# Retention and a token-mixing MLP on one core: a table-driven order, its engines, banks and load forms written anew

## The chip, the cores and the metric

The kernel runs on one core of a Trainium2 chip. The metric is the device time of the kernel in microseconds. Before the change the median of three runs is 100.91 us (100.23, 100.91 and 100.99).

## What is computed

Four batches of 768 tokens, eight heads of 64 channels. The first half is retention, a decayed recurrent attention; the second a mixing MLP whose token-mixing weights come from the tokens themselves:

```python
state = gamma * state + k[t] (outer) v[t]          # per head, gamma_h = 1 - 2**(-5-h)
y[t]  = (1/8) * q[t] @ state                       # retention
x     = y, heads side by side                      # (batch, 768, 512)
wq, wk = x @ w_q, x @ w_k                          # 64 wide
mixed = (wq @ wk.T / 8) @ x                        # per batch, no softmax
out   = relu(mixed) @ w_out
```

## The kernel before

The work is cut into 12 *pairs*: a pair is two chunks of 128 tokens of one batch, three pairs make a batch. Within a pair retention is computed by chunks: products of q and k under a causal mask (the decay is put into v and into the output as row factors), plus q times the state that the earlier chunks left. The mixing is reassociated: z = wk^T x is summed over the three pairs of a batch, then mixed = wq z, so a batch's mixing waits for its three pairs.

All five engines are scheduled by hand. One table, ORDER, is a list of tokens that a loop at the kernel's end turns into instructions, so the order of tokens is the order of each engine's own queue. A token `name.pair.part:E@banks=slot` names the step, the engine E (A = ACT, V = DVE, P = POOL; steps without it run on PE) and the PSUM banks. A semaphore wait is made where a step reads what another engine or a DMA writes, or overwrites what is still read; each engine works through its queue strictly in order. The steps of a pair:

- Lk, Lq, Lv (L172 to L193): load k, q, v (512 KB each, fp32) into one of 27 staging slots; all but half of the first v are issued by SP. LW and LO load the MLP's weights; S stores.
- ck, cq, cv (L351, L408, L375): cast k and q to bf16, and multiply v by its decay factor into bf16 (cv, on POOL).
- trk, trq, xt (L448, L505, L710): PE transposes into PSUM, as eight 128x128 ones into one bank or, with two banks named, sixteen 64-row ones. ek, eq, exT copy the result to SBUF.
- sc, eat (L533, L568): PE scores of one half of the heads, then DVE multiplies by the mask.
- st, es (L585, L601): PE adds k^T v of a chunk to the state in bank 7; es copies the state to SBUF. A chunk's st must wait until es has read the state before it.
- in, ia, ex (L623, L661, L694): PE adds q times state and scores times v; DVE scales by the decay into x.
- wqk, ew, zm, ez, mx (L744 to L798): the two small projections (matmuls at L748 and L759), their copy, z, its copy, and the mixing.
- r, pj, eo (L814, L823, L835): relu of one chunk, projection by w_out (four matmuls at L826), copy into a staging slot.
- fill (L345) puts matmuls on zeros into PE's queue where it would stand idle.

KINDS gives each pair's layout of k and v. "R": two neighbouring tokens lie side by side in a partition (512-byte rows); the cast then sorts chunks into partition halves, so ck takes two 64-partition instructions for each chunk, and cv too. "2" keeps the two tokens side by side: ck and cv are one 128-partition instruction for each part, but sc, in and ia need twice the PE instructions, on quarters of the array (L544, L641, L652). "M": k as in R, v loaded as 256-byte rows, four DMAs for each pair (L185), so that cv is one 128-partition instruction for each chunk. Before, pairs 1, 2 and 6 are "2" and pairs 9, 10 and 11 "M".

BUFS gives the number of buffers of each tile. A step that takes a new tile waits until all readers of the one it replaces are done. relu had four tiles of one chunk each.

Of the kernel before, what the change touches and what calls it, by code (L numbers as in the profile page):

```python
# [22 lines left out]
Lq.10=5 cv.3.1:P cq.5.0:P ia.0.1@56 fill.1@1 trk.2@1 fill.1@3 in.0.1@56 Lk.10=12 cq.2.1:A cq.2.0:A
sc.1.0@23 ek.2:V cv.4.0:P sc.1.1@01 trq.2@4 eq.2:A es.0.1:A ia.0.0@56 eat.1.0:V ex.0:V eat.1.1:V
cv.4.1:P fill.4@2 sc.2.1@34 cq.3.0:A cv.5.0:P sc.2.0@56 fill.2@2 st.1.0 es.1.0:A ck.3.0:A ck.3.1:A
Lv.10=6 Lq.11=8 ia.1.1@01 in.1.1@01 st.1.1 eat.2.1:V ck.6.0:P ia.1.0@01 in.1.0@01 trq.3@4 eat.2.0:V
xt.0@5 cv.5.1:P ex.1:V cq.7.1:P cq.7.0:P cv.6.1:P es.1.1:V exT.0:V eq.3:V trk.3@6 fill.2@2 in.2.0@01
cv.6.0:P Lv.11=9 st.2.0 ck.4.1:A ek.3:A xt.1@5 es.2.0:A exT.1:V ck.4.0:A ia.2.1@01 ia.2.0@01
in.2.1@01 ck.7.1:P ex.2:V st.3.0 fill.1@2 sc.3.0@56 trk.4@34a cq.4.1:A cv.7.1:P cv.7.0:P W:A trq.4@0
xt.2@1 ek.4:V sc.3.1@23 ck.8.1:P cq.8.0:P eat.3.0:V eq.4:V wqk.1@4 ew.1:V cq.5.1:A exT.2:A es.3.0:A  # L30
wqk.0@5 ck.8.0:P sc.4.0@01 trq.5@6 wqk.2@4 ck.5.1:A ew.0:A eat.4.0:V ew.2:V zm.0.0@5 sc.4.1@01
st.3.1 eat.3.1:V ck.5.0:A WO.0:A es.3.1:A trk.5@4 cq.9.1:P cv.8.0:P in.3.1@23 zm.0.1@5 ia.3.1@23
ia.3.0@23 eat.4.1:V ez.0:V cv.9.0:P cv.8.1:P st.4.0 ex.3:V ek.5:A es.4.0:A in.4.0@01 mx.0@45
in.4.1@01 ia.4.1@01 ia.4.0@01 eq.5:V WO.1:A st.4.1 xt.3@23a r.0.1:A pj.0.1@6 ex.4:V r.0.0:A es.4.1:A
ck.6.1:A eo.0.1:A=11 xt.4@01a cv.9.1:P mx.1@45 exT.3:V r.1.0:A cq.6.0:A sc.5.0@23 pj.0.0@6 st.5.0
exT.4:V r.1.1:V eat.5.0:V trk.6@4 ek.6:V sc.5.1@01 cq.6.1:A eo.0.0:A=11 trq.6@56a wqk.4@2 es.5.0:A
ia.5.0@34 eq.6:A in.5.0@34 in.5.1@34 eat.5.1:V trq.7@56a mx.2@01 ew.4:V eq.7:V r.2.1:A r.2.0:A
ck.7.0:A ia.5.1@34 wqk.3@2 ex.5:V pj.1.0@5 sc.6.1@01 st.6.0 eo.1.0:A=14 sc.6.0@34 xt.5@6 trk.7@5
ek.7:A eat.6.1:V pj.1.1@0 exT.5:V wqk.5@6 es.6.0:V st.6.1 eo.1.1:A=14 ew.5:A es.6.1:A ew.3:A
# [6 lines left out]
cv.11.0:P cq.10.1:A xt.6@12a in.8.1@34 in.8.0@34 mx.5@56 eq.9:A cv.11.1:P ia.8.0@34 ia.8.1@34
wqk.7@0 exT.6:V r.5.0:A r.5.1:A sc.9.0@12 sc.9.1@56 cq.10.0:A ex.8:V eat.9.0:V st.9.0 trq.10@3
ew.7:A pj.5.0@0 trk.10@12a wqk.6@4 eat.9.1:V ia.9.0@56 ia.9.1@56 ck.11.1:A es.9.0:A S.3 ek.10:V
eo.5.0:A=18 eq.10:A in.9.1@56 xt.8@01a sc.10.1@23 st.9.1 exT.8:A ew.6:V pj.4.1@4 trk.11@0 es.9.1:A
ex.9:V wqk.8@1 eat.10.1:V trq.11@23a ek.11:A sc.10.0@56 st.10.0 ew.8:A zm.2.0@0 es.10.0:A  # L50
eo.4.1:A=16 eq.11:V eat.10.0:V zm.2.1@0 ez.2:A st.10.1 xt.9@12a sc.11.1@34 pj.5.1@0 eat.11.1:V
exT.9:A es.10.1:A ia.10.0@56 mx.6@12 sc.11.0@34 eat.11.0:V in.10.1@56 in.10.0@56 eo.5.1:A=18 st.11.0
r.6.0:A ia.10.1@56 pj.6.0@0 r.6.1:A ex.10:V es.11.0:A ia.11.1@34 ia.11.0@34 eo.6.0:A=17 in.11.0@34
in.11.1@34 mx.8@12 xt.10@56a r.8.0:A exT.10:A S.4 r.8.1:V wqk.9@0 pj.8.1@1 mx.7@56 S.2 ex.11:V
ew.9:A eo.8.1:V=19 xt.11@23a exT.11:A pj.8.0@0 wqk.10@1 eo.8.0:A=19 ew.10:A wqk.11@2 ew.11:V r.7.1:V
S.1 pj.6.1@0 zm.3.0@1 eo.6.1:A=17 zm.3.1@1 ez.3:V r.7.0:V pj.7.1@2 mx.9@01 mx.11@34 mx.10@56
eo.7.1:A=21 r.9.1:V pj.7.0@2 r.9.0:A pj.9.1@0 r.10.0:A pj.9.0@1 S.8 S.5 eo.7.0:A=21 r.11.1:A
pj.11.1@2 S.6 eo.9.0:V=22 r.11.0:A r.10.1:A pj.10.1@6 S.7 S.9.0 pj.11.0@1 eo.10.1:V=20 eo.9.1:A=22
eo.11.1:A=23 pj.10.0@0 eo.10.0:A=20 eo.11.0:V=23 S.9.1 S.11.1 S.10.1 S.11.0 S.10.0
""".split()  # L60

KINDS = "R22RRR2RRMMM"
FIRST = ('v', 0, 0)
SLOTS = 27
U = 8
PAD = 224
SPLIT = ()
# [9 lines left out]
def kernel(  # L77
# [270 lines left out]

    def ck(e, b, p, c):  # L351
        st = pairs[p]
        if KINDS[p] in "2H":
            if "ks" not in st:
                st["ks"] = new("ks", [128, HP, 2, 2, D])
            copy(
                e,
                st["ks"][:, :, :, c],
                st["k_st"].rearrange("p (hp x j d) -> p hp x j d", hp=HP, x=2, j=2)[:, :, c],
            )  # L360
            return
        if "ks" not in st:
            st["ks"] = new("ks", [128, 2, HP, 2, D])
        if KINDS[p] == "N":
            copy(
                e,
                st["ks"][:, c].rearrange("p hp x d -> p (hp x d)"),
                st["k_st"][:, 512 * c : 512 * c + 512],
            )
            return  # L370
        src = st["k_st"].rearrange("p (h j d) -> p h j d", j=2, d=D)
        for j in range(2):
            copy(e, st["ks"][rows(j), c].rearrange("p hp x d -> p (hp x) d"), src[rows(c), :, j])
# [31 lines left out]
                op=ALU.mult,  # L405
            )

    def cq(e, b, p, x):  # L408
        st = pairs[p]
        if U == 8:  # L410
            if "qs" not in st:
                st["qs"] = new("qs", [128, U, 2, D])
            copy(e, st["qs"][:, :, x], st["q_st"].rearrange("p (x u d) -> p x u d", x=2, u=U)[:, x])
# [90 lines left out]

    def trq(e, b, p):  # L505
        st = pairs[p]
        qs = st["qs"]
        ident = ident_q if U == 8 else identity
        srcs = [(None, u) for u in range(U)] if U == 8 else [(hp, u) for hp in range(HP) for u in range(U)]
# [12 lines left out]
    def eq(e, b, p):  # L522
        st = pairs[p]
        st["qT"] = new("qT", [128, 2, HP, C])
        b = st["qtr"]
        if len(b) == 1:
            copy(e, st["qT"].rearrange("p c hp t -> p (c hp t)"), bank16(b[0]))
        else:
            copy(e, st["qT"].rearrange("p c hp t -> p c (hp t)"), two16(b))
# [281 lines left out]
                )  # L811
        st["mx_ps"] = ps

    def r(e, b, p, c):  # L814
        st = pairs[p]
        st["relu", c] = new("relu", [128, 2, 2, C])
        src = st["mx_ps"][:, :, :, c * C : c * C + C]
        if e == "A":
            nc.scalar.activation(out=st["relu", c], in_=src, func=ACT.Relu)  # L819
        else:  # L820
            nc.vector.tensor_relu(out=st["relu", c], in_=src)  # L821

    def pj(e, b, p, c):  # L823
        st = pairs[p]
        for a in range(NDM):
            nc.tensor.matmul(  # L826
                out=bank32(b[0]),
                lhsT=st["relu", c][:, a // 2, a % 2, :],
                rhs=wout_sb[:, a, :],
                start=(a == 0),  # L830
                stop=(a == NDM - 1),
# [69 lines left out]
```

## Time and profile before

| | us |
|---|---|
| median of three runs | 100.91 |
| the profiled execution, its own time | 100.14 |
| its span in the profile | 98.4 |
| PE busy | 88.6 |
| DVE busy | 74.4 |
| ACT busy | 70.3 |
| POOL busy | 51.8 |

The profiled execution is 1.7 us longer than its span: that lies around the span and no engine's work is in it. Busy times of PE are those of pipelined matmuls, whose ends overlap the next one's start; what a step costs PE is better read from the chain of waits, where each piece begins where the one before ends. The granted clock is 0.996 over the span. In the profile, a row names line, engine, operation, output and inputs; "[0.89 <-DMA stage<-in_v_dram]" says that the engine stood idle for 0.89 us before the row and that a load of v ended the wait. SPq rows are DMA issues and last as long as SP is held by them.

### The profile page before, as it was taken

Reading aid. Unit: us, or ns where it says so; the run is one execution under the profiler, and the core shown is the slowest. Engines: PE = TensorE matmul, PEld = TensorE weight load, DVE = VectorE, ACT = ScalarE, POOL = GpSimd, SP = SyncE. Lnnn points to the kernel's source line nnn. Section 1 sums busy time; section 2 is a strip of 40 time slices with the busy share of each in tenths; the row PEclk is TensorE's granted clock in tenths of the full one; section 3 lists DMA queues with packets and bytes.
Section 4 is the critical chain, followed back from the end, with each engine's and each line's share of the span. In section 5 each row is a group of like instructions: output and inputs, shape, how many; then the busy total and the mean of one; then the engine's idle time right before and its main releaser. Section 6 shows DMA issues by size and latency. Waiting matters only on the chain.

```text
span 98.4 us, 3827 instructions
## 1 busy us (share of the span) xinstructions
PE 88.6 (90%) x1626; PEld 59.9 (61%) x1642; DVE 74.4 (76%) x127; ACT 70.3 (71%) x124; POOL 51.8 (53%) x68
## 2 busy tenths in 40 slices
PE   5994899999869999999999988999999989999940
PEld 1333477487757776586887554786787766744410
DVE  6697689999792999998769897888958964460440
ACT  4237573689799979967589967899579776339620
POOL 6082319176385989989977999497990000000000
PEclk9999999999999999999999999999999999999998
DMA  1999999999998999999899799799905910690893
GB/s 26 282 385 368 367 363 361 343 327 282 293 330 256 303 317 348 354 336 293 255 337 309 177 323 323 159 244 273 361 21 205 402 46 0 245 391 14 323 397 132
DMA packets 37953, 26.73 MB, mean 272 GB/s; under 512 B 8240, under 2 KB 31792, under 8 KB 37936
## 3 DMA queue, kind: packets, MB, share of 16 engines
q1 hardware_dynamic: 37408, 26.22, 84.5%
q10 hardware_dynamic: 528, 0.26, 0.9%
q8 instruction: 13, 0.21, 0.8%
q14 instruction: 4, 0.03, 0.1%
HBM read 20.19 MB, written 6.29 MB: 269 GB/s over the span
## 4 chain that ended last, share of the span: by engine, by line
PE 55%; SPq 20%; ACT 7%; DMA 6%; DVE 4%; issue 2%; POOL 1%; DVEq 0%; POOLq 0%
PE banks L826 19%; SPq L193 11%; DMA stage<-in_q_dram 6%; SPq L172 6%; PE banks L748 5%; PE banks L759 5%; PE banks L558 3%; PE banks L685 3%; SPq L200 3%; ACT relu L819 3%; PE banks L592 2%; PE banks L515 2%; PE banks L804 2%; DVE relu L821 2%; PE banks L631 2%
## 5 line engine op out<-in xcount | busy, mean ns | idle before, releaser
L401 POOL TENSOR_TENSOR vs<-stage,fv 64x512 bf16<-64x512 f32 x22 | 23.6, 1075 | 6.4 <-DMA stage<-in_v_dram 5.2
L576 DVE TENSOR_TENSOR at<-banks,maskR 128x1024 bf16<-128x1024 f32 x18 | 21.7, 1219 | 3.8 <-PE banks L558 3.8
L826 PE MATMUL banks<-wout_sb,relu 128*128 128x512 bf16 x84 | 22.9, 381 | 0.9 <-DVE relu L821 0.2
L147 ACT CAST ks<-stage 64x512 bf16<-64x512 f32 (+1 forms) x25 | 15.4, 618 | 4.7 <-DMA stage<-in_k_dram 4.3
L147 ACT COPY stage<-banks 128x512 f32<-128x512 f32 x19 | 11.0, 587 | 5.8 <-PE banks L826 5.7
L706 DVE TENSOR_TENSOR x<-banks,fy 128x1024 bf16<-128x1024 f32 x12 | 14.6, 1219 | 0.6 <-PE banks L685 0.3
L826 PEld LDWEIGHTS <-relu 128*128 128x128 bf16 x96 | 8.3, 99 | 9.3 <-issue 0.8
L148 POOL CAST ks<-stage 64x512 bf16<-64x512 f32 (+1 forms) x15 | 9.1, 609 | 6.4 <-DMA stage<-in_k_dram 5.8
L347 PE MATMUL banks<-warm 128*128 128x512 bf16 x34 | 10.9, 451 | 1.6 <-DVE warm L226 1.2
L819 ACT ACTIVATE relu<-banks 128x512 bf16<-128x512 f32 x18 | 10.0, 601 | 3.0 <-PE banks L804 1.5
L147 ACT CAST qs<-stage 128x512 bf16<-128x512 f32 x14 | 8.4, 618 | 1.5 <-DMA stage<-in_q_dram 1.3
L382 POOL TENSOR_TENSOR vs<-stage,fv 128x512 bf16<-128x512 f32 x6 | 6.2, 1047 | 5.4 <-DMA stage<-in_v_dram 5.4
L576 DVE TENSOR_TENSOR at<-banks,mask 128x1024 bf16<-128x1024 f32 x6 | 7.1, 1219 | 1.0 <-ACT ks L147 0.8
L147 ACT COPY kT<-banks 128x1024 bf16<-128x1024 bf16 x6 | 6.1, 1011 | 2.4 <-PE banks L473 1.7
L759 PE MATMUL banks<-wqk_w,xT 128*128 128x64 bf16 x96 | 7.5, 243 | 0.1
L558 PE MATMUL banks<-qT,kT 64*128 64x128 bf16 x144 | 6.8, 218 | 0.9 <-ACT kT L147 0.5
L347 PEld LDWEIGHTS <-warm 128*128 128x128 bf16 x38 | 3.8, 110 | 6.0 <-issue 3.0
L147 ACT CAST s<-banks 128x256 bf16<-128x256 f32 x16 | 6.0, 375 | 1.9 <-PE banks L592 1.9
L748 PE MATMUL banks<-xT,wqk_w 128*128 128x256 bf16 x48 | 7.3, 275 | 0.0
L148 DVE COPY qT<-banks 128x1024 bf16<-128x1024 bf16 x8 | 5.5, 686 | 2.0 <-PE banks L515 1.0
L148 POOL CAST qs<-stage 128x512 bf16<-128x512 f32 x9 | 5.4, 611 | 2.8 <-DMA stage<-in_q_dram 2.5
L592 PE MATMUL banks<-vs,ks 128*64 128x64 bf16 (+1 forms) x200 | 6.9, 198 | 0.0
(81 smaller groups left out, 153.4 us busy)
## 6 DMA issues: line engine op xcount, KB each, us to landing
stage<-in_k_dram SPq DMA_DIRECT2D x12, 512.0 KB, 7.4
stage<-in_q_dram SPq DMA_DIRECT2D x12, 512.0 KB, 6.6
out_dram<-stage SPq DMA_DIRECT2D x9, 512.0 KB, 4.0
stage<-in_v_dram SPq DMA_DIRECT2D x8, 512.0 KB, 7.8
stage<-in_v_dram SPq DMA_DIRECT2D x12, 128.0 KB, 5.2
out_dram<-stage SPq DMA_DIRECT2D x6, 256.0 KB, 2.2
stage<-in_moe_w_out_dram SPq DMA_DIRECT2D x4, 256.0 KB, 4.8
stage<-in_v_dram ACTq DMA_DIRECT2D x1, 256.0 KB, 4.3
```

The costliest lines, as they stand in the source:

```text
L147: return nc.scalar.copy(out=out, in_=in_)
L148: return ENGINES[e].tensor_copy(out=out, in_=in_)
L193: eng.dma_start(out=to[g, hs], in_=fr[g, hs])
L347: nc.tensor.matmul(out=bank32(b), lhsT=warm[:, 0:128], rhs=warm, start=True, stop=True)
L401: eng.tensor_tensor(out=st["vs"][rows(j), c].rearrange("p hp x d -> p (hp x) d"), in0=src[rows(c), :, j], in1=fv[rows(c), cp, :, j].to_bro ...
L558: nc.tensor.matmul(out=at[:, x, hi, c], lhsT=kT[rows(x), hp, c], rhs=qT[rows(x), c, hp], start=(hi == 0 and c == 0), stop=(hi == 1 and c = ...
L576: ENGINES[e].tensor_tensor(out=st["at", half].rearrange("p x hi j t -> p x (hi j t)").rearrange("p x (n f) -> p x n f", n=n), in0=st["at_p ...
L706: ENGINES[e].tensor_tensor(out=dst, in0=src, in1=f.to_broadcast([128, 2, H, D]), op=ALU.mult)
L748: nc.tensor.matmul(out=ps[:, 128:384], lhsT=wqk_sb[:, a, 0 : 2 * DH], rhs=st["xT"][:, a].rearrange("p c t -> p (c t)"), start=(a == 0), st ...
L759: nc.tensor.matmul(out=wk[:, c], lhsT=st["xT"][:, a, c, :], rhs=wqk_sb[:, a, 2 * DH :], start=False, stop=(a == NDM - 1), skip_group_check ...
L819: nc.scalar.activation(out=st["relu", c], in_=src, func=ACT.Relu)
L826: nc.tensor.matmul(out=bank32(b[0]), lhsT=st["relu", c][:, a // 2, a % 2, :], rhs=wout_sb[:, a, :], start=(a == 0), stop=(a == NDM - 1),)
```

## The change

Four things change.

1. ORDER is another table: the order of steps on all engines, the engine of many steps, the PSUM banks, the order of loads, the slots, and the number and places of the fillers (43 for 38).
2. KINDS: pair 1 alone is "2"; pair 2 is "R"; pairs 6 and 7 are "M" like 9, 10 and 11. Pairs 0, 3, 4, 5 and 8 stay "R".
3. ck, cq and r may take both parts in one instruction. It is used for ck of pair 1 and cq of pairs 2, 7 and 9 on POOL, cq of pairs 1, 4, 5 and 6 on ACT, and r of pairs 1, 3, 4, 7 and 8 on ACT.
4. relu becomes one tile for a whole pair, and there are two of them.

A switch QF (transposing q in fp32) is added and left empty.

```diff
-fill.15@6 cv.0.0:V Lk.0=1 ck.0.1:V Lq.0=2 ck.0.0:A Lq.1=3 Lk.1=4 Lk.2=5 Lq.2=6 Lv.1=7 fill.3@0
...
+fill.15@6 Lk.0=1 cv.0.0:V ck.0.0:P Lq.0=2 cq.0.0:V cv.0.1:P Lk.1=3 ck.0.1:A Lq.1=4 Lq.2=5 Lk.2=6
+Lv.1=7 Lq.3=8 fill.7@0 trk.0@0 ek.0:V Lv.2=9 ck.1:P cq.0.1:A Lk.3=10 st.0.0 trq.0@1 eq.0:V fill.3@2
...
-KINDS = "R22RRR2RRMMM"
+KINDS = "R2RRRRMMRMMM"
...
-    ks=6, vs=6, qs=4, kT=3, qT=3, at0=2, at1=2, s=4, x=6, xT=3, m=7, z=2, relu=4,
+    ks=6, vs=6, qs=4, kT=3, qT=3, at0=2, at1=2, s=4, x=6, xT=3, m=7, z=2, relu=2,
...
-    def ck(e, b, p, c):
+    def ck(e, b, p, c=None):
...
+            if c is None:
+                copy(
+                    e,
+                    st["ks"].rearrange("p hp j x d -> p hp x j d"),
+                    st["k_st"].rearrange("p (hp x j d) -> p hp x j d", hp=HP, x=2, j=2),
+                )
+                return
...
-    def cq(e, b, p, x):
+    def cq(e, b, p, x=None):
...
+            if x is None:
+                copy(
+                    e,
+                    st["qs"].rearrange("p u x d -> p x u d"),
+                    st["q_st"].rearrange("p (x u d) -> p x u d", x=2, u=U),
+                )
+                return
...
-    def r(e, b, p, c):
-        st = pairs[p]
-        st["relu", c] = new("relu", [128, 2, 2, C])
-        src = st["mx_ps"][:, :, :, c * C : c * C + C]
+    def r(e, b, p, c=None):
+        st = pairs[p]
+        if "relu" not in st:
+            st["relu"] = new("relu", [128, 2, 2, 2 * C])
+        ts = slice(0, 2 * C) if c is None else slice(c * C, c * C + C)
+        dst, src = st["relu"][:, :, :, ts], st["mx_ps"][:, :, :, ts]
...
-                lhsT=st["relu", c][:, a // 2, a % 2, :],
+                lhsT=st["relu"][:, a // 2, a % 2, c * C : c * C + C],
```

Three places of the new order follow, as the built programs have it. The first is DVE at its first real work, after the constants. (vs, ks and qs are the bf16 tiles of v, k and q, kT and qT the transposed ones, at the masked scores, x the retention's output.) Before:

```order
L401 TENSOR_TENSOR vs_206<-stage_110,fv_158 64x512 x2
L148 CAST ks_210<-stage_110 64x512 x2
L148 CAST qs_236<-stage_110 128x8x64
L148 COPY qT_271<-banks_109 128x1024
L148 COPY kT_273<-banks_109 128x1024
L576 TENSOR_TENSOR at1_356<-banks_109,maskR_183 128x1024
```

And now:

```order
L414 TENSOR_TENSOR vs_207<-stage_110,fv_158 64x512 x2
L148 CAST qs_214<-stage_110 128x8x64
L148 COPY kT_241<-banks_109 128x1024
L148 COPY qT_264<-banks_109 128x1024
L610 TENSOR_TENSOR at0_310<-banks_109,maskR_183 128x1024
L610 TENSOR_TENSOR at1_316<-banks_109,maskR_183 128x1024
```

The cast of pair 0's k has left DVE (POOL has it now, ahead of its first product), and kT goes before qT.

The second is SP's queue of loads, from v of pair 1, the eighth tensor, on. Before:

```order
L193 DMA stage<-in_v_dram 128x8x128
L172 DMA stage<-in_q_dram 128x2x512
L193 DMA stage<-in_k_dram 128x8x128
L193 DMA stage<-in_v_dram 128x8x128
L193 DMA stage<-in_k_dram 128x8x128
L193 DMA stage<-in_v_dram 128x8x128
L200 DMA stage<-in_moe_w_q_dram 128x4x64
L200 DMA stage<-in_moe_w_k_dram 128x4x64
L172 DMA stage<-in_q_dram 128x2x512 x2
```

And now:

```order
L193 DMA stage<-in_v_dram 128x8x128
L172 DMA stage<-in_q_dram 128x2x512
L193 DMA stage<-in_v_dram 128x8x128
L193 DMA stage<-in_k_dram 128x8x128 x2
L193 DMA stage<-in_v_dram 128x8x128
L172 DMA stage<-in_q_dram 128x2x512
L200 DMA stage<-in_moe_w_q_dram 128x4x64
L200 DMA stage<-in_moe_w_k_dram 128x4x64
L193 DMA stage<-in_v_dram 128x8x128
```

v of pair 2 goes ahead of k of pair 3, and q of pair 4 ahead of the weights. Ahead of this piece, k of pair 2 went from sixth to seventh. Further on, v of pairs 6 and 7 are four DMAs each (64x8x64), the second of them the 27th tensor.

The third is ACT around the relu of pair 2. Before, with relu tiles of one chunk:

```order
L147 COPY qT_1188<-banks_109 128x1024
L819 ACTIVATE relu_1232<-banks_109 128x512
L819 ACTIVATE relu_1234<-banks_109 128x512
L147 CAST ks_755<-stage_110 64x512 x2
L147 COPY stage_110<-banks_109 128x512
```

And now, where the first of DVE's and ACT's halves takes the tile:

```order
L147 COPY stage_110<-banks_109 128x512
L855 ACTIVATE relu_1065<-banks_109 128x4x128
L147 CAST s_1069<-banks_109 128x256
L147 CAST ks_1071<-stage_110 64x512 x2
L147 CAST qs_1076<-stage_110 128x2x8x64
```

Behind pair 2's relu there now stand the copy of pair 5's state and the casts of k and q of pair 6.

More of the change, by code (lines that the diff above doesn't have):

```diff
@@ L23 @@
[L23 to L39, printed above, removed]
@@ L46 @@
[L46 to L51, printed above, removed]
@@ new lines @@
+eo.1.1:A=3 ez.1:A st.6.0 Lv.8=7 eq.8:V eat.7.1:V ek.8:V es.6.0:A mx.3@45 sc.7.0@01 in.6.1@23
+eat.7.0:V Lq.11=8 r.3:A Lk.11=10 st.6.1 ia.6.0@23 ia.6.1@23 ck.9.0:A cv.8.0:P cv.8.1:P pj.3.0@4
+sc.8.1@01 mx.5@56 eo.3.0:A=9 es.6.1:V ex.6:V Lv.9=11 st.7.0 eat.8.1:V r.5.0:V trk.9@4 es.7.0:A
+ek.9:A ck.11.0:P pj.3.1@2 xt.6@3 exT.6:V r.5.1:A ia.7.1@01 cv.9.1:P ia.7.0@01 eo.3.1:A=9 mx.4@45
+in.7.0@01 Lk.10=13 r.4:A in.7.1@01 trq.9@23a st.7.1 Lq.10=14 wqk.6@6 ex.7:V eq.9:V es.7.1:A
+cq.11.0:A cv.9.0:P ck.10.1:P ew.6:A pj.5.0@4 sc.8.0@01 xt.7@56a Lv.10=12 eo.5.0:A=16 exT.7:A
@@ L306 @@
         )
+    if QF:
+        ident_f = const_pool.tile([128, 128], FP32, name="ident_f")
+        nc.vector.tensor_copy(out=ident_f, in_=ident_q)
     def mask(name, toks):
@@ L506, in trq @@
         st = pairs[p]
+        if p in QF:
+            src = st["q_st"].rearrange("p (x u d) -> p u x d", x=2, u=U)
+            st["qtr"] = ps = two32(b).rearrange("p i (v n) -> p i v n", n=C)
+            for u in range(U):
+                nc.tensor.transpose(ps[:, u // 4, u % 4], src[:, u], ident_f)
+            return
         qs = st["qs"]
```

69 lines of the change are left out of this document (48 added, 21 removed).

## Prediction

> **What bounds the kernel now.** I read the page first: engines, slices, queues.
>
> ```profile
> span 98.4 us, 3827 instructions
> ...
> PE   5994899999869999999999988999999989999940
> ...
> DMA  1999999999998999999899799799905910690893
> ...
> q8 instruction: 13, 0.21, 0.8%
> ```
>
> PE is nearly full from the third slice on, and DMA is full for two thirds of the span. Thirteen instruction reads took 0.8% of 16 engines' span, 0.008 x 16 x 98.4 / 13 = 0.97 us each on one DMA engine, which a load split over all engines waits for. The chain of waits shows where one limit gives way to the other.
>
> ```profile
> 20.97 6.24 DMA stage<-in_q_dram
> ...
> 27.32 0.62 POOL qs L148
> ...
> 27.99 0.62 PE banks L515 x8
> ...
> 29.39 0.54 PE banks L748 x4
> ...
> 33.34 0.56 DVE m L148
> 33.90 1.14 DVE at L576
> ...
> 92.71 1.90 PE banks L826 x8
> 94.64 0.58 ACT stage L147
> ```
>
> Until 27.2 us the chain is loads: q of pair 4 lands, POOL casts it, PE transposes it (L515), and only behind that, at 29.39, starts the first L748 matmul (the hypernetwork weights, token wqk.1). From there to 94.61 the chain is nearly all PE. So I ask three things: when does wqk.1 start, how much PE work stands behind it, and what makes PE wait there.
>
> **PE work behind wqk.1.** The same view gives what each step costs PE when it is not waiting.
>
> ```profile
> 38.11 0.34 PE banks L721 x16
> ...
> 46.83 0.35 PE banks L544 x16
> ...
> 51.18 0.22 PE banks L558 x8
> ...
> 51.86 0.12 PE banks L641 x4
> 51.98 0.24 PE banks L652 x8
> ...
> 63.24 0.23 PE banks L631 x16
> ...
> 69.38 0.23 PE banks L721 x16
> ...
> 71.05 0.45 PE banks L473 x8
> ```
>
> Behind wqk.1 the tables hold the same 24 pj, 12 mx, 12 wqk and 8 zm. Pair 6 loses the two-token form: two halves of sc fall from 0.35 to 0.22 (L544 to L558), -0.26; a row of in from 0.12 + 0.24 to half of 0.23, -0.24. (Pair 2 loses it too, ahead of wqk.1, where PE runs fillers: nothing.) Four xt go from sixteen half-height transposes (0.23 and 0.34, mean 0.28) to eight full ones (0.45, as in L473): +0.68. One trq moves behind wqk.1, half-height, taken like the other 16-transpose rows at 0.23. Sum -0.26 - 0.24 + 0.68 + 0.23 = +0.4 us.
>
> **When wqk.1 starts.** These timeline rows of DVE, ACT and POOL give durations and landings (a wait on a DMA ends when it has landed).
>
> ```profile
> 5.04 2.14 DVE L401 TENSOR_TENSOR vs<-stage,fv 64x512 bf16<-64x512 f32 x2 [0.89 <-DMA stage<-in_v_dram]
> 7.19 1.61 DVE L148 CAST ks<-stage 64x512 bf16<-64x512 f32 x2
> ...
> 12.05 1.23 DVE L576 TENSOR_TENSOR at<-banks,maskR 128x1024 bf16<-128x1024 f32 x1 [0.50 <-PE banks L558]
> ...
> 16.14 1.22 DVE L576 TENSOR_TENSOR at<-banks,mask 128x1024 bf16<-128x1024 f32 x1
> 17.29 1.23 DVE L706 TENSOR_TENSOR x<-banks,fy 128x1024 bf16<-128x1024 f32 x1
> ...
> 25.93 1.23 DVE L706 TENSOR_TENSOR x<-banks,fy 128x1024 bf16<-128x1024 f32 x1 [0.24 <-PE banks L652]
> ```
>
> ```profile
> 6.54 1.25 ACT L147 CAST ks<-stage 64x512 bf16<-64x512 f32 x2 [3.42 <-DMA stage<-in_k_dram]
> ```
>
> ```profile
> 5.24 2.85 POOL L401 TENSOR_TENSOR vs<-stage,fv 64x512 bf16<-64x512 f32 x2 [2.98 <-DMA stage<-in_v_dram]
> ...
> 14.99 2.05 POOL L382 TENSOR_TENSOR vs<-stage,fv 128x512 bf16<-128x512 f32 x2 [2.21 <-DMA stage<-in_v_dram]
> ...
> 20.34 2.05 POOL L382 TENSOR_TENSOR vs<-stage,fv 128x512 bf16<-128x512 f32 x2 [2.74 <-DMA stage<-in_v_dram]
> 23.21 2.16 POOL L401 TENSOR_TENSOR vs<-stage,fv 64x512 bf16<-64x512 f32 x2 [0.82 <-DMA stage<-in_v_dram]
> ```
>
> ```profile
> L147 ACT CAST ks<-stage 64x512 bf16<-64x512 f32 x22 | 13.6, 616 | 3.7 <-DMA stage<-in_k_dram 3.4
> ...
> L147 ACT COPY kT<-banks 128x1024 bf16<-128x1024 bf16 x6 | 6.1, 1011 | 2.4 <-PE banks L473 1.7 <-PE banks L457 0.5 <-DVE at L576 0.2
> ...
> L148 DVE COPY qT<-banks 128x1024 bf16<-128x1024 bf16 x8 | 5.5, 686 | 2.0 <-PE banks L515 1.0 <-PE banks L519 1.0
> ```
>
> Loads land in queue order: k of pair 0, the second tensor, at 6.5, the eighth at 14.9, the eleventh at 20.3, the thirteenth at 23.1. Eighth less second is 8.4 / 6 = 1.4 us a tensor. From eighth to eleventh 5.4 us stand for three, 1.2 more than 4.2: one instruction read (0.97) fits. PE has 3080 rows for 3286, so twelve reads for thirteen, at most 0.97 us; I count none of it, since by PE's place in its queue the first two reads still fall among tensors ten to fourteen.
>
> Now I add rows along the new order. k of pair 0 is cast by POOL and ACT from 6.54 (1.25 each) instead of ACT and DVE, whose own 2.14 and 1.61 went first: its transposes end at 8.6, DVE's two copies (0.69 each) at 10.0, the first eat starts at 10.5 (12.05 now), and x of pair 0 at 13.4 (17.29). Then the lead is spent: k of pair 2 is seventh, 13.4, its casts end at 14.7, and PE has trk.2 and trq.2 ahead of sc.1.0, so the first eat of pair 1 starts near 16.0 (16.14). k of pair 3 has become eleventh, 20.3; ACT casts it and half of pair 4's in 3 x 1.25 to 24.05, es.1.1 stands behind, in.2.0 waits for that, and x of pair 2 starts at 25.9 (25.93). So up to here nothing is won, though early steps move by over 1.5 us. The gain comes after it: trq.4 now stands behind wqk.1, so PE doesn't wait for q of pair 4. x of pair 2 ends at 27.1, xt.2 at 27.65, one filler follows; ACT has copied xT of pair 1 by 25.2 and, after q of pair 4 (a 1024-wide cast taken at the 1.01 of a 1024-wide copy), cast the weights by 27.05. wqk.1 starts at 27.85: -1.5 us. Bounds: 0, if anything on ACT slips to where q's landing was; -2.4, if the third read falls later and k of pair 3 lands 0.97 earlier.
>
> POOL's cast of k of pair 1 in one 1024-wide piece, and q of pair 2, have no row on POOL; between 1.01 (ACT's 1024-wide copy) and twice 0.62 (the 64x512 row), taken at 1.15; either end leaves k of pair 2, landing at 13.4, as what PE waits for.
>
> Where DVE's first k cast met POOL's product, its two halves took 1.61 us (ACT's two 1.25), and POOL's two products 2.85 against 2.16 later. In the Trainium skill, "SBUF — State Buffer", section "Who interferes with whom", a DVE cast in a two-port mode and a GpSimd instruction exclude each other: the later one is blocked for the whole instruction. The trace agrees in kind. By that rule the new DVE cast of q of pair 0, at 7.8, waits for POOL's next product, 1.0 us, and the first eat of pair 1 starts at 16.4 in place of 16.0; the sum below would be -0.5 if that were carried on, and stays at -0.9 by the rows, as the wait for k of pair 3 at 20.3 comes after it.
>
> **What makes PE wait behind wqk.1.** Before, PE stands 1.7 us at 33.34 for DVE's m and at. In the new order these are done when in.3.1 and zm.0.0 come (31.6): -1.7. Smaller new waits in the same stretch, added up along the rows (mx for ez, pj for WO.0, st.5.0 for v): +0.85. The new one that I find is the relu tile: two whole tiles for two pairs, so that pair 2's r waits until both projections of pair 0 are done. ACT is in order: r.2.0 waits for pj.0.0 (near 40.0), behind it stand es.5.0, k and q of pair 6 (0.4 + 1.25 + 1.0), to 43.1, and trq.6 on PE, free at 42.1, waits for that q: +1.05. Merged casts and relus save ACT some 0.1 us each; they are inside these times. Together +0.2. Later waits I leave as they are: at the tail the last relus wait on projections just ended, about 0.1 each.
>
> **256-byte rows.** POOL saves two of four products on pair 7; the loads pay.
>
> ```profile
> 48.06 6.27 SPq L185 DMA_DIRECT2D stage<-in_v_dram  x4
> ```
>
> ```profile
> 12.00:16.00 4.00, 3.84 (x80) 2.87 (x80) 3.64 (x4) 2.77 (x4) 1.63 (x3) 1.00 1.08 372
> 54.00:57.00 3.00, 3.00 (x65) 1.85 (x65) 2.71 (x4) 2.87 (x6) 2.87 (x5) 1.00 0.80 182
> ```
>
> ```profile
> 52.16 1.26 POOL L148 CAST ks<-stage 64x512 bf16<-64x512 f32 x2 [0.96 <-DMA stage<-in_k_dram]
> ```
>
> 0.524 MB at 372 GB/s is 1.4 us, at the 182 of such a stretch 2.9: +1.5 at most, 0 at least; I take 1.3. The 27th tensor, which landed at 52.2, is now v of pair 7, behind a second such load: 54.8. Its product ends near 55.9, and st.7.0 needs it at 56.7. Hidden, by 0.8 us.
>
> **Sum.** -1.5 + 0.4 + 0.2 = -0.9 us on the profiled execution of 100.14 (span 98.4): 99.2. That run lies 0.77 below the median of three, 100.91; the same step from the median gives 100.0. I take the middle, 99.6.
>
> **Rivals.** (1) *The lead isn't there.* wqk.1 starts near 29.4, since DVE and ACT, not loads, pace the front: x of pair 2 comes out no earlier in my own sum. Then 99.6 + 1.5 = 101.1. Against it: what PE waits for at 27.99 is a load's cast. (2) *Slower: SP is held by the 256-byte rows.* Four issues kept SP 6.27 us, and what is queued behind them started late. If a load costs 6.0 instead of 2.7, v of pair 7 lands 6.6 later, the slack takes 0.8, and PE stands 5.8 at st.7.0: 105.4. It makes the kernel slower by over 1% (above 101.9) from 3.1 us of delay on. Against: SP may only have waited for room. (3) *Slower: the relu tile.* Two tiles also hold r.9 behind both projections of pair 6 and r.11 behind those of pair 10, at the end, where nothing covers PE. If each costs one projection (four L826 matmuls; the eight from 92.71 took 1.90, so 0.95), +1.9 and another 0.5 at r.2: 102.0. Against: in the order other pairs' projections stand between.
>
> **Chances.** Forecast 0.55 (own range 98.2 to 100.6), of which 0.13 falls within 1%; rival 1 0.16, within 1%, of which 0.02 slower; rival 2 0.10, rival 3 0.19, slower. A measurement can tell about 1% from no change. Faster by over 1%: 0.55 - 0.13 = 0.42; within: 0.13 + 0.14 = 0.27; slower: 0.02 + 0.10 + 0.19 = 0.31. The range leaves out rival 2's far end and the forecast's early tail: 98.2 to 102.6.
>
> **What would show it.** Right: the first L748-kind matmul near 27.9, not 29.4; x of pair 2 still near 26; ACT idle before relu of pair 2, released by PE, near 40; PE idle before the transposes of pair 6. Wrong: PE waiting on POOL's v of pair 7 or 8 (rival 2), or on ACT or DVE relu in the last 6 us (rival 3). My sums along the rows take about 0.1 us for a hand-over between engines; were it 0.2 throughout the front, the lead would go.

## The result, and the profile after

The changed kernel takes 103.75 us (median of four runs, 102.56 to 104.01) where the kernel before, beside it, takes 100.89 (100.23 to 100.99): a ratio of 1.035, interval 1.029 to 1.041. The forecast was 99.6, its range ended at 102.6, and the sign was the other one. Ratios here leave disturbed runs out, so that one of them need not be the quotient of two medians. The profiled execution took 103.8 us, its span is 102.0, and its mean granted clock 0.983 where it was 0.996.

The slices of the page, 2.55 us each, show where to look.

```profile
span 102.0 us, 3618 instructions
...
PE   5997699799999999918999999999999999999650
...
PEclk9999999999999999995899999999999999999999
DMA  1999999999999979997999995996910693267764
...
q8 instruction: 12, 0.20, 0.8%
```

PE has one hole, the 18th slice (43.4 to 45.9 us), and in the two slices behind it the granted clock is down. Windows of PE, PEld, DVE, ACT and POOL, with the clock, the DMA share and GB/s at the end of a row, put numbers to it.

```profile
42.00:44.00 2.00, 1.43 (x31) 0.97 (x32) 1.54 (x3) 0.96 (x3) 1.22 (x3) 1.00 1.06 381
44.00:46.00 2.00, 0.24 (x8) 0.12 (x7) 1.23 (x1) 1.96 (x3) 0.70 (x1) 0.94 1.09 293
46.00:48.00 2.00, 1.63 (x19) 0.93 (x21) 0.69 (x1) 1.95 (x4) 1.10 (x3) 0.50 0.80 171
48.00:50.00 2.00, 2.00 (x30) 1.39 (x30) 0.00 (x0) 1.50 (x4) 1.94 (x3) 0.70 0.81 235
50.00:52.00 2.00, 2.00 (x58) 1.68 (x51) 1.79 (x4) 1.96 (x4) 1.17 (x3) 1.00 1.11 250
```

PE is busy 0.24 us of two, then for four microseconds nearly full but at a mean clock of 0.50 and 0.70: 19 and 30 matmuls in the time in which it then does 58 (different ones, but the same L782 matmuls that take 0.60 a group elsewhere take 1.00 here). The 0.70 is a mean of two values; cut at other places, the windows show one step down and one up:

```profile
45.00:45.75 0.75, 0.00 (x0) 0.00 (x0) 0.50 (x1) 0.73 (x2) 0.46 (x1) 1.00 1.10 268
45.90:49.00 3.10, 2.63 (x22) 1.49 (x24) 0.69 (x1) 3.03 (x6) 2.14 (x4) 0.50 0.71 163
49.25:50.00 0.75, 0.75 (x25) 0.65 (x25) 0.00 (x0) 0.28 (x2) 0.75 (x1) 1.00 1.15 337
```

The timeline of PE says whom it waited for.

```profile
43.95 0.29 PE L665 MATMUL banks<-s,qT 64*128 64x64 bf16 x8 [0.52 <-ACT s L147]
46.15 0.61 PE L545 MATMUL banks<-ident_q,qs 64*128 64x64 bf16 x16 [1.91 <-ACT qs L147]
...
47.52 1.06 PE L862 MATMUL banks<-wout_sb,relu 128*128 128x512 bf16 x2 [0.22 <-issue]
48.38 1.00 PE L782 MATMUL banks<-xT,wqk_w 128*128 128x256 bf16 x4
```

The transposes of q of pair 6 (trq.6, L545) wait 1.91 us for ACT's cast. ACT's timeline shows what came before that cast, and DVE's what ACT had waited for.

```profile
39.38 0.59 ACT L147 COPY stage<-banks 128x512 f32<-128x512 f32 x1 [0.71 <-POOL vs L414]
43.04 0.60 ACT L855 ACTIVATE relu<-banks 128x512 bf16<-128x512 f32 x1 [3.07 <-DVE relu L857]
43.53 0.37 ACT L147 CAST s<-banks 128x256 bf16<-128x256 f32 x1
43.78 1.25 ACT L147 CAST ks<-stage 64x512 bf16<-64x512 f32 x2
45.05 1.04 ACT L147 CAST qs<-stage 128x1024 bf16<-128x1024 f32 x1
```

```profile
39.99 2.36 DVE L610 TENSOR_TENSOR at<-banks,maskR 128x1024 bf16<-128x1024 f32 x2
42.26 0.68 DVE L857 TENSOR_SCALAR relu<-banks 128x512 bf16<-128x512 f32 x1
```

ACT stands 3.07 us before its half of pair 2's relu, r.2.0, and it is not released by PE near 40, as the prediction had it, but by DVE's half, r.2.1. That half stands in DVE's queue behind two masks of pair 5 (2.36 us) and comes at 42.26. Behind r.2.0 on ACT are the state and the casts of k and q of pair 6 (0.37, 1.25, 1.04), exactly the queue that the prediction named.

At the end of the kernel a second new wait shows, in ACT's timeline first and then in PE's.

```profile
95.16 0.60 ACT L855 ACTIVATE relu<-banks 128x512 bf16<-128x512 f32 x1 [1.20 <-PE banks L862]
```

```profile
92.32 3.40 PE L862 MATMUL banks<-wout_sb,relu 128*128 128x512 bf16 x15 [0.23 <-DVE relu L857]
96.54 1.90 PE L862 MATMUL banks<-wout_sb,relu 128*128 128x512 bf16 x8 [0.83 <-ACT stage L147]
```

r.11.1 waits 1.20 us for the projections of pair 10, and PE then stands 0.83 us before the last eight matmuls. The front, last, came out much as it was walked. These are DVE's rows and the first projection of pair 1 on PE (wqk.1).

```profile
8.01 1.13 DVE L148 CAST qs<-stage 128x512 bf16<-128x512 f32 x1 [1.77 <-DMA stage<-in_q_dram]
...
14.10 1.23 DVE L740 TENSOR_TENSOR x<-banks,fy 128x1024 bf16<-128x1024 f32 x1
...
16.44 2.36 DVE L610 TENSOR_TENSOR at<-banks,mask 128x1024 bf16<-128x1024 f32 x2 [0.53 <-PE banks L578]
...
26.51 1.22 DVE L740 TENSOR_TENSOR x<-banks,fy 128x1024 bf16<-128x1024 f32 x1
```

```profile
28.52 0.60 PE L782 MATMUL banks<-xT,wqk_w 128*128 128x256 bf16 x4
```

k of pair 3, for which ACT waits, landed at 20.1:

```profile
20.07 3.78 ACT L147 CAST ks<-stage 64x512 bf16<-64x512 f32 x6 [1.64 <-DMA stage<-in_k_dram]
```

The same view of the kernel before has wqk.1 and the last projections here:

```profile
29.32 0.61 PE L748 MATMUL banks<-xT,wqk_w 128*128 128x256 bf16 x4
...
88.08 6.52 PE L826 MATMUL banks<-wout_sb,relu 128*128 128x512 bf16 x27
```

(The chain of waits gave 29.39 for the same start, because there a piece begins where the one before ends.) So wqk.1 starts 0.8 us earlier than before, and the loss lies wholly behind it: from there to the end of the last projection it is 98.44 - 28.52 = 69.9 us, before 94.60 - 29.32 = 65.3.

### The profile page after: what moved, and what is told of

The parts are those of the page before. It is cut to its first block, busy times and chain, and to the rows that moved or that the text cites. A ratio compares the mean times of both kernels' runs of the same rounds, so it can differ in the third digit from the quotient of the medians.

```text
span 102.0 us, 3618 instructions
## 1 busy us (share of the span) xinstructions
PE 89.7 (88%) x1524; PEld 61.1 (60%) x1539; DVE 74.4 (73%) x128; ACT 68.3 (67%) x112; POOL 54.8 (54%) x70
## 4 chain that ended last, share of the span: by engine, by line
PE 49%; SPq 34%; DMA 6%; ACT 4%; issue 3%; DVE 1%; ACTq 0%
SPq L193 19%; PE banks L862 18%; SPq L172 12%; DMA stage<-in_q_dram 6%; PE banks L782 5%; PE banks L793 4%; PE banks L592 4%; PE banks L719 3%; SPq L207 2%; PE banks L626 2%; PE banks L838 2%; PE banks L819 2%; PE banks L493 2%; PE banks L545 1%; PE banks L665 1%
## 5 line engine op out<-in xcount | busy, mean ns | idle before, releaser
L862 PE MATMUL banks<-wout_sb,relu 128*128 128x512 bf16 x85 | 23.6, 389 | 1.9 <-ACT stage L147 0.8
L147 ACT CAST ks<-stage 64x512 bf16<-64x512 f32 x26 | 16.0, 616 | 7.0 <-DMA stage<-in_k_dram 6.7
L862 PEld LDWEIGHTS <-relu 128*128 128x128 bf16 x96 | 8.3, 101 | 9.4 <-issue 1.5
L855 ACT ACTIVATE relu<-banks 128x512 bf16<-128x512 f32 (+1 forms) x12 | 9.2, 778 | 4.6 <-DVE relu L857 3.1
L405 POOL TENSOR_TENSOR vs<-stage,fvm 128x512 bf16<-128x512 f32 x10 | 10.2, 1043 | 3.8 <-DMA stage<-in_v_dram 3.7
L147 ACT CAST qs<-stage 128x512 bf16<-128x512 f32 (+1 forms) x10 | 7.9, 794 | 2.2 <-DMA stage<-in_q_dram 2.1
L148 DVE COPY kT<-banks 128x1024 bf16<-128x1024 bf16 x8 | 5.5, 685 | 3.3 <-PE banks L499 2.6
L782 PE MATMUL banks<-xT,wqk_w 128*128 128x256 bf16 x48 | 7.7, 286 | 0.0
L592 PEld LDWEIGHTS <-kT 64*128 64x128 bf16 x176 | 5.3, 94 | 3.5 <-issue 2.5
L719 PE MATMUL banks<-vs,at 128*128 128x64 bf16 x176 | 7.2, 194 | 0.1
L148 POOL CAST qs<-stage 128x1024 bf16<-128x1024 f32 (+1 forms) x6 | 5.0, 825 | 3.4 <-DMA stage<-in_q_dram 3.0
L147 ACT COPY qT<-banks 128x1024 bf16<-128x1024 bf16 x5 | 5.1, 1016 | 2.5 <-PE banks L545 1.4
L719 PEld LDWEIGHTS <-at 128*128 128x128 bf16 x176 | 6.1, 98 | 0.9 <-issue 0.2
```

What stands on the lines that cost most here:

```text
L147: return nc.scalar.copy(out=out, in_=in_)
L148: return ENGINES[e].tensor_copy(out=out, in_=in_)
L592: nc.tensor.matmul(out=at[:, x, hi, c], lhsT=kT[rows(x), hp, c], rhs=qT[rows(x), c, hp], start=(hi == 0 and c == 0), stop=(hi == 1 and c = ...
L719: nc.tensor.matmul(out=y[:, x, c, hp, :], lhsT=at[:, x, hi, c, :], rhs=vr[:, c, hp, x, :], start=first(p, x), stop=False, skip_group_check ...
L782: nc.tensor.matmul(out=ps[:, 128:384], lhsT=wqk_sb[:, a, 0 : 2 * DH], rhs=st["xT"][:, a].rearrange("p c t -> p (c t)"), start=(a == 0), st ...
L862: nc.tensor.matmul(out=bank32(b[0]), lhsT=st["relu"][:, a // 2, a % 2, c * C : c * C + C], rhs=wout_sb[:, a, :], start=(a == 0), stop=(a = ...
```

## The experiments

Why does ACT wait for DVE's relu, when the two halves are different elements of the same tile, computed from different columns of the same two banks? Theory A: because of the relu tile. It is now one tile for both chunks; the second engine to write into it waits for the first. Theory A2: because of the banks. Both halves read the mixing result of pair 2 from banks 0 and 1, and the program lets two engines read a bank only one after the other, in the order in which the table names them; the new table names DVE's half first. Rivals for the loss as a whole: the number of relu tiles (two for pairs), and the 256-byte rows.

**The tile laid out with each chunk in one piece.** The kernel after, with

```diff
-            st["relu"] = new("relu", [128, 2, 2, 2 * C])
+            st["relu"] = new("relu", [128, 2, 2, 2, C])
...
-                lhsT=st["relu"][:, a // 2, a % 2, c * C : c * C + C],
+                lhsT=st["relu"][:, c, a // 2, a % 2, :],
```

> The new order with its two relu tiles, but the two chunks of a tile lie one behind the other instead of interleaved. Theory A (the halves of one interleaved tile wait for each other: ACT's half of pair 2's relu stood 3.07 us behind DVE's half of the same tile, PE then stood 1.91 us before the transposes of q of pair 6, the granted clock fell to 0.50, and at the tail three relus stood in a row): ACT's relu of pair 2 starts when the last projection of pair 0 ends, near 41.3 instead of 43.04, PE's stand falls below 0.7 us, the clock stays at 1.0, and the time is 103.75 - 1.5 - 1.2 (slow clock) - 0.8 (tail) = 100.2 (99.6 to 101.0). Theory B (two tiles are too few, whatever their layout): within 0.5 us of 103.75. Theory C (256-byte rows): within 0.5 us of 103.75.

103.32 us, ratio to before 1.0293 (1.0194 to 1.0391), and ACT's wait is the same:

```profile
42.55 0.60 ACT L858 ACTIVATE relu<-banks 128x512 bf16<-128x512 f32 x1 [3.07 <-DVE relu L860]
```

That the halves interleave in the tile is not the reason.

**Three relu tiles.** The kernel after, with `relu=3` for `relu=2`.

> The new order with three relu tiles instead of two, still interleaved. Theory A: ACT still stands behind DVE's half; 103.2 to 104. Theory B: the wait goes with the third tile; 100 to 101.5. Theory C: within 0.5 us of 103.75.

102.83 us, 1.0269 (1.0188 to 1.035). ACT still waits 3.01 us for DVE's relu, at 42.75. The number of tiles does not make that wait. The time lies between what the theories had forecast (103.2 to 104 and 100 to 101.5): the third tile takes away the wait at the tail, where the last 23 matmuls now run through, and leaves the one in the middle.

**Pairs 6 and 7 back in 512-byte rows.**

```diff
-KINDS = "R2RRRRMMRMMM"
+KINDS = "R2RRRRRRRMMM"
```

> The new order with pairs 6 and 7 in form R again (v in 512-byte rows; POOL then has four half-height products for each instead of two). Theory C (the 256-byte rows of v of pairs 6 and 7 hold up SP and the loads behind them, and with them PE): 101 to 102.5. Theories A and B: the wait at 43 us is ahead of these loads' use, so 103.2 to 104.5, a little slower if POOL's 2.1 us more a pair show.

103.66 us, 1.0345 (1.0254 to 1.0436), the same as the kernel after (1.035), with ACT's 3.07 us wait in place. The 256-byte rows are not the loss.

**One relu tile for a pair, in the old order.** The kernel before, with its relu written into one tile for a pair, three of them.

> The order before, with nothing changed but the relu tiles: one interleaved tile for a pair, three of them, in place of four tiles of one chunk. Theory A: pairs 1, 4, 8 and 9, whose chunks are on ACT and DVE, wait for each other; 0.3 to 1.2 us slower than before, 101.2 to 102.1. Theory B (three tiles suffice): 100.9, no change. If it is no change, the interleaved tile hurts only where the two engines are far apart.

100.52 us, 1.0016 (0.9972 to 1.0061). In the old order the shared tile costs nothing that can be told. This doesn't yet part A from A2, since in the old order both halves of pair 2's relu were on ACT.

**ACT's half first.** The kernel after with two tokens exchanged. Each engine's queue stays word for word as it was; what turns round is who waits for whom.

```diff
-... ck.8.1:P cq.8.1:P r.2.1:V
-eo.1.0:V=3 r.2.0:A es.5.0:A ...
+... ck.8.1:P cq.8.1:P r.2.0:A
+r.2.1:V eo.1.0:V=3 es.5.0:A ...
```

> The new order with one pair of tokens exchanged, ACT's half of pair 2's relu named ahead of DVE's half. Every engine's queue stays as it was; only who waits for whom changes, since two engines that read the same two PSUM banks are made to read one after the other in the order of the table. Theory A2 (that wait, not the tile's layout, cost 3.07 us on ACT): ACT's relu starts when the last projection of pair 0 ends, near 41.3 instead of 43.0; PE's 1.9 us stand before the transposes of q of pair 6 falls below 0.8; with that the clock does not fall; 103.4 - 1.7 - 1.2 = 100.5 (99.8 to 101.3). Theory B (only the third tile helps) and theory D (the order as a whole is worse, this wait only hides other waits): 102.5 or more.

100.59 us, 1.0035 (1.0006 to 1.0063), as the theory of the banks had it, and the clock stays at 1.00. ACT and PE now:

```profile
40.96 0.60 ACT L855 ACTIVATE relu<-banks 128x512 bf16<-128x512 f32 x1 [1.48 <-PE banks L862]
```

```profile
44.07 0.41 PE L545 MATMUL banks<-ident_q,qs 64*128 64x64 bf16 x16 [1.02 <-ACT qs L147]
...
93.06 1.90 PE L862 MATMUL banks<-wout_sb,relu 128*128 128x512 bf16 x8 [0.83 <-ACT stage L147]
```

The exchange of two names is worth 3.2% of the time (1.035 to 1.0035). What is left of the wait is the one that the prediction had: r.2.0 for PE's projections (L862), 1.02 us at trq.6, more than the 0.8 that I had allowed. The wait at the tail is unchanged.

**ACT's half first, and three relu tiles.** Both edits together.

> The exchange of e5 and three relu tiles. Theory A2 with the tile wait on top: ACT's relu of pair 2 starts right behind the copy before it, near 39.9; PE doesn't stand there; and at the tail ACT's relu of pair 11 no longer waits for both projections of pair 10 (1.20 us of ACT, 0.83 of PE): 99.6 (98.8 to 100.5). If the tile count were worth nothing: as e5.

98.57 us, 0.9835 (0.9776 to 0.9893): faster than both kernels, and a little below the expected range. ACT's r.2.0 does not wait, PE does not stand before trq.6, and the tail runs through:

```profile
39.87 0.60 ACT L855 ACTIVATE relu<-banks 128x512 bf16<-128x512 f32 x1
```

```profile
43.38 0.40 PE L545 MATMUL banks<-ident_q,qs 64*128 64x64 bf16 x16
...
88.12 5.34 PE L862 MATMUL banks<-wout_sb,relu 128*128 128x512 bf16 x23 [0.23 <-DVE relu L857]
```

**Fillers in the hole.** The kernel after, its wait left as it is, with eight matmuls on zeros ahead of trq.6 (`fill.8@3 trq.6@01a`), to part the standing from the slow clock behind it.

> The new order with eight filler matmuls in PE's queue just before the transposes of q of pair 6, where PE stands; nothing else changes, and the wait itself stays. If the fall of the granted clock to 0.5 follows from PE standing still: the clock stays near 1.0 behind the hole, and the time is 103.4 - 1.2 = 102.2 (101.8 to 102.8). If the clock falls for another reason, or the work behind it waits for ACT anyway: within 0.4 us of the new order's time.

102.12 us, 1.0203 (1.0151 to 1.0255). ACT waits 3.07 us as before, trq.6 comes at 45.91, but the clock holds:

```profile
46.00:48.00 2.00, 1.84 (x31) 1.43 (x31) 0.69 (x1) 1.95 (x3) 1.60 (x3) 1.00 0.69 175
```

So 1.035 - 1.0203 = 1.5% of the loss is the clock, and 1.0203 - 1.0035 = 1.7% the longer standing. The executions without a trace bear the price of the clock out. Of the four of the version with each chunk in one piece, three had a mean clock of 0.976 or 0.977 and took 103.24 to 103.56 us; the fourth had 1.000 and took 102.16. Of the four of the kernel after, the one of 102.56 us had 0.993, the others 0.980 to 0.983. So by these clocks the same stand does not bring the clock down every time, and where it did not the time is 1.1 to 1.5 us shorter; no trace shows those two executions.

**The new order with a tile for each chunk.** DVE's half still named first, but each half in a tile of its own, six of them, as the kernel before had it (a merged r becomes two instructions).

```diff
-            st["relu"] = new("relu", [128, 2, 2, 2 * C])
+        st["relu", c] = new("relu", [128, 2, 2, C])
```

> The new order with DVE's half of pair 2's relu still named first, but each half in a tile of its own (six tiles), as in the kernel before. Theory of the bank order (ACT may read mx of pair 2 only after DVE has, because both read the same two banks and the program lets them in one after the other in the table's order): ACT's r.2.0 still waits about 3 us on DVE's relu, with its start at 42 to 43.5, and the time is 102 to 103, as with three pair tiles (102.8). Rival, the shared pair tile (a tile that two engines write lets the second wait): ACT's wait is gone, r.2.0 starts by 41, and the time is 98.5 to 100.5.

102.77 us, 1.0249 (1.0178 to 1.0321).

```profile
42.70 0.60 ACT L857 ACTIVATE relu<-banks 128x512 bf16<-128x512 f32 x1 [3.01 <-DVE relu L859]
```

No tile is shared, and the wait is there; what the two relus still have in common is banks 0 and 1. Theory A falls; with the exchange above, A2 stands: the wait hangs on the order in which the two readers of the banks are named, and on nothing about the tile.

The next four start from the faster version (ACT's half first, three tiles, 98.57) and test the prediction's other steps.

**512-byte rows for pairs 6 and 7 in that version.** The same edit of KINDS.

> The version with ACT's half first and three relu tiles (98.57), with v of pairs 6 and 7 in 512-byte rows. If the 256-byte rows are hidden by slack, as the prediction had it, the time is within 0.5 us of 98.6. If they save POOL time that the engines behind it wait for, it is 99.2 to 100.5; if they cost DMA time that something waits for, 97 to 98.

98.86 us, 0.9852 (0.9786 to 0.9918) where the version itself has 0.9835: no difference that can be told.

**The transposes of q of pair 4 ahead of the first projection.** `trq.4@01a wqk.1@3` for `wqk.1@3 trq.4@01a`.

> The same version with the transposes of q of pair 4 ahead of the first projection of pair 1, as they stood before. They need the bank that eat.3.0 frees (its end is at 28.9), so wqk.1 starts near 29.3 to 29.6 instead of 28.5. If the lead in front reaches the end, the time is 0.5 to 1.1 us above 98.6; if a later wait swallows it, within 0.3 us of 98.6.

98.82 us, 0.9855 (0.9777 to 0.9934), again not told from 0.9835. PE's timeline:

```profile
28.51 0.41 PE L545 MATMUL banks<-ident_q,qs 64*128 64x64 bf16 x16 [0.31 <-DVE at L610]
28.85 0.61 PE L782 MATMUL banks<-xT,wqk_w 128*128 128x256 bf16 x4
```

With the transposes first, wqk.1 starts at 28.85, earlier than the 29.3 to 29.6 that I expected and 0.3 us or more later than in the other versions; the time does not show it, since the stretch behind wqk.1, without these transposes, is 64.5 us for 64.9. They wait 0.31 us for a bank, not for q.

**Pair 0's second product on DVE.** POOL then runs nothing while DVE casts q of pair 0.

```diff
-fill.15@6 Lk.0=1 cv.0.0:V ck.0.0:P Lq.0=2 cq.0.0:V cv.0.1:P Lk.1=3 ...
+fill.15@6 Lk.0=1 cv.0.0:V ck.0.0:P cv.0.1:V Lq.0=2 cq.0.0:V Lk.1=3 ...
```

> The version with ACT's half first and three relu tiles, with the second half of v of pair 0 multiplied on DVE (free from 6.1 to 8.0) instead of POOL, so that POOL runs nothing while DVE casts q of pair 0. If the cast took 0.8 to 1.25 us because POOL's product ran beside it, it now takes 0.43 and ends by 8.6, and the first mask of pair 1 starts at 15.7 to 16.1 instead of 16.2 to 16.8. If that delay was carried on to the projections (x of pair 2 is held by the chain from those masks), x of pair 2 starts at 25.9 to 26.1 instead of 26.0 to 26.5, wqk.1 at 27.8 to 28.1, and the time is 0.2 to 0.6 us below the control. If the landing of k of pair 3 takes over, as the prediction had it, x of pair 2 and the time stay within 0.2 us of the control.

98.72 us, 0.9837 (0.978 to 0.9894). Its control:

> The control on the same chip: the version with ACT's half first and three relu tiles as it was. Both theories: 98.3 to 98.9; cast of q of pair 0 0.8 to 1.25 us, first mask of pair 1 at 16.2 to 16.9, wqk.1 at 28.0 to 28.5.

98.73 us, 0.9838 (0.978 to 0.9896): no difference. The cast itself did what was expected. DVE in the version with the product moved, and then in the control:

```profile
8.65 0.43 DVE L148 CAST qs<-stage 128x512 bf16<-128x512 f32 x1 [0.67 <-DMA stage<-in_q_dram]
...
16.99 2.35 DVE L610 TENSOR_TENSOR at<-banks,mask 128x1024 bf16<-128x1024 f32 x2 [1.02 <-PE banks L578]
```

```profile
7.64 1.31 DVE L148 CAST qs<-stage 128x512 bf16<-128x512 f32 x1 [1.54 <-DMA stage<-in_q_dram]
...
16.25 2.35 DVE L610 TENSOR_TENSOR at<-banks,mask 128x1024 bf16<-128x1024 f32 x2 [0.53 <-PE banks L578]
```

The cast took 0.43 us for 1.31. But in that execution q had landed 1.0 us later (8.65 for 7.64), which undid the gain, so the first mask of pair 1 came later, not earlier. My expectation of 0.2 to 0.6 us less was a miss. Whether the later landing came from the edit or only from that execution is open: the same front in the other experiments has this cast start anywhere from 7.6 to 8.3.

The trace of the version with three tiles alone shows the same thing without an edit. There the cast began just ahead of POOL's product, and the product came second. DVE, then POOL:

```profile
7.69 0.43 DVE L148 CAST qs<-stage 128x512 bf16<-128x512 f32 x1 [1.45 <-DMA stage<-in_q_dram]
```

```profile
7.74 2.39 POOL L414 TENSOR_TENSOR vs<-stage,fv 64x512 bf16<-64x512 f32 x2
```

Its first mask of pair 1 starts at 16.02, the earliest of these traces, and yet its x of pair 2 only at 26.28. The version with ACT's half first and 512-byte rows has them at 16.60 and 26.09. A late first mask does not by itself make x of pair 2 late.

## Why the prediction was wrong, step by step

The steps can be set against two stretches: up to the start of wqk.1, and from there to the end of the last projection (the last row of L862 matmuls).

| | wqk.1 starts | from there to the end of the last projection |
|---|---|---|
| before | 29.3 | 65.3 |
| forecast (27.85; 65.3 + 0.4 + 0.2) | 27.9 | 65.9 |
| after | 28.5 | 69.9 |
| ACT's half first | 28.0 | 66.9 |
| ACT's half first, three tiles | 28.5 | 64.9 |

**When wqk.1 starts: -1.5 forecast, -0.8 measured.** The sign was right. The walk had x of pair 0 at 13.4, the first mask of pair 1 at 16.0 and x of pair 2 at 25.9; measured were 14.1, 16.44 and 26.51. The prediction weighed a rule there: the Trainium skill, "SBUF — State Buffer", section "Who interferes with whom", by which a two-port DVE cast and a GpSimd instruction exclude each other. The trace agrees: the cast of q of pair 0 took 1.13 us beside POOL's product and 0.43 without it, and the first mask came at 16.44, where the rule had put it (16.4). Where the cast came ahead of the product, the first mask came at 16.02, as the rows without the rule had it (16.0). I left that delay out of the sum, because the wait for k of pair 3 was to swallow it. Over the traces of this front that holds: the first mask starts anywhere from 16.0 to 16.8, and x of pair 2 from 26.0 to 26.5, not in the same order. What keeps x of pair 2 0.1 to 0.6 us behind the walk's 25.9, in the kernel after although k of pair 3 had landed at 20.1, in time, is open. wqk.1 lies from 28.0 to 28.5 in these traces (28.85 with the transposes ahead of it), so the walk was 0.2 to 0.7 us too early.

The reason that I gave for the gain was wrong. I let it come from trq.4 being put behind wqk.1. Put ahead again, it loses nothing that can be told. What PE had waited for at 27.99 before, POOL's cast of q of pair 4, is gone in either place: that load now stands ahead of the weights and landed at 25.5 in the experiment, where before it had landed at 27.2, and ACT casts it.

**PE work behind wqk.1: +0.4.** Not measured by itself. The trq that moved behind wqk.1 was taken at 0.23; in the kernel after the next group starts 0.34 us after it (29.49 to 29.83).

**What makes PE wait: +0.2 forecast, and here the prediction failed.** It has three parts.

The first was -1.7, "before, PE stands 1.7 us at 33.34 for DVE's m and at". PE didn't stand. The chain of waits passes through DVE there, but that only says that the last releaser of a later PE step was DVE. Windows of the same stretch, of the kernel before and then of the kernel after:

```profile
31.00:36.00 5.00, 4.79 (x89) 3.60 (x87) 3.89 (x4) 4.73 (x8) 3.86 (x4) 1.00 0.98 280
```

```profile
31.00:36.00 5.00, 4.80 (x101) 3.74 (x99) 4.03 (x5) 4.15 (x9) 4.47 (x6) 1.00 1.01 292
```

PE is busy 4.79 of 5.00 us before and 4.80 after, and no filler is among it: there was no 1.7 to win. Nor were there +0.85 of new waits to lose: from wqk.1 to 43 us the kernel after has two waits of PE for other engines, of 0.2 us each. That the two and the +0.4 sum to -0.45, and that the version without r.2.0's waits and the wait at the tail has a stretch shorter by 0.3 (65.3 to 64.9), is then partly luck.

The second was +1.05, r.2.0 waiting for pj.0.0 because of two tiles. This was right, and only hidden behind a longer wait: with that gone, PE stands 1.02 us at trq.6, and with a third tile nothing.

The third is the step that was missing. I asked, for r.2.0, what it waits for on PE and in the tile, and did not ask who else reads its banks. In the order of the kernel after ACT's r.2.0 waits for DVE, and in the version with the exchange DVE's r.2.1 waits for ACT; the built programs differ in that. By exchange, it costs 69.9 - 66.9 = 3.0 us: in place of 1.02 PE stands 0.52 + 1.91 + 0.22 = 2.65 us, 1.6 more, and the rest is the slow clock behind it. A page states the reason for the program's care: the Trainium skill, "PSUM — Partial Sum Buffer", section "PSUM bank collisions raise a hardware error", says that two different engines must not be in one bank, on the same partitions, at once, even when both only read, and that software has to order them with semaphores. The trace agrees that they are ordered (3.07 us of ACT's time); what an unordered pair would do no run here shows. Read before predicting, that sentence would have sent me to every place where the new table gives the halves of one bank to two engines, and to the question which of them is named first. The kernel before had such places too, with a tile for each chunk. Its waits, in us in total, times and the longest:

```profile
ACT relu L819 <- DVE relu L821: 1.4, 2, 0.9
```

They were in the trace that I had, and their cause went unasked.

I also left out that a PE that stands costs clock. The Trainium skill, "TensorE: Matmul & The Clock Gate", section "What's actually happening", has the clock fall to half after an idle window of about 3.4 us. Here it fell to 0.50 at 45.8, when PE had stood 2.1 of some 2.4 us (0.52 and the first 1.5 of 1.91, with 0.29 of matmuls between), sooner than a whole idle window would have it, and it stayed at 1.00 after 1.02 us of standing, and with fillers in the hole.

**The tail.** "At the tail the last relus wait on projections just ended, about 0.1 each" was the other missed term: r.11.1 waits 1.20 us, PE 0.83. Rival 3 had named this place and the cause, two tiles; it priced it at 1.9, over twice what was measured. With r.2.0, two tiles cost 66.9 - 64.9 = 2.0 us in all. Rival 3's total of 102.0 had the direction right without containing the main cause.

**256-byte rows: hidden.** Right, twice (103.66 for 103.75, 98.86 for 98.57). Rival 2, SP held by them, is out.

So the last projection ends 98.44 - 94.60 = 3.8 us later: rounded, -0.8 in front, +3.0 for the turned order of two readers with its slow clock, +2.0 for two relu tiles, -0.3 for all the rest. How the 5.0 of the two middle terms divides hangs on which is taken away first, since one wait hides behind the other: with three tiles alone the stretch is 97.64 - 28.29 = 69.35, so the third tile is then worth 0.6 and the exchange 4.4. The forecast held the first term and about half of the third; it was sunk by the second and by the tail. With the second and third taken away the change makes the kernel 1.65% faster (0.9835).

## What to carry to other kernels

Where a program built like this one lets two engines each read a part of one PSUM bank, the engine that it names second waits for the first, and so for all that stands ahead in the first one's queue: name the engine first that is free first, and when an order is moved, go over every such pair again, in both directions. A step in the chain of waits that belongs to another engine is not idle time of PE; before counting it as a gain, look at PE's busy time in that window. And a stand of PE like this one, 0.5 and 1.9 us in close succession, should be priced with the slow clock that may follow it, here about 1.5 us more, or filled.

## What the runs showed of the hardware

Two things I had not expected. First, the clock: in all five traces where the hole of 0.5 and 1.9 us before trq.6 is not filled, the granted clock went from 1.00 to 0.50 once, stayed there for 3.41 us and went back to 1.00. It fell anywhere from 0.4 us before PE went on to 0.95 us after, so that part of the slow time can lie well behind the hole that caused it. Eight matmuls on zeros in the hole, which are no work, gave back 1.5% of the kernel's time.

Second, DVE and POOL slow each other in both directions, and what counts is who began first. In the ten traces where DVE's cast of q of pair 0 began 0.02 to 0.68 us after POOL's product, it took 1.31 to 0.65 us and always ended 1.32 or 1.33 us after the product began; where it began 0.05 us before the product, or where POOL ran none, it took 0.43. And when the product was moved to DVE, where it ran beside POOL's cast of k of pair 0, that cast took 2.07 us for 1.27 in the control:

```profile
6.38 2.07 POOL L148 CAST ks<-stage 64x512 bf16<-64x512 f32 x2 [4.12 <-DMA stage<-in_k_dram]
```

```profile
6.27 1.27 POOL L148 CAST ks<-stage 64x512 bf16<-64x512 f32 x2 [4.00 <-DMA stage<-in_k_dram]
```
